# Channel attention and a silu FFN on one core: v's maxima by quarters, halves scaled by two blocks at fixed places, output joins behind subtractions, squares behind copies, the second attention later, decoding held back

## The chip, the cores and the metric

One core of a Trainium2 chip runs one program. The time is device time in microseconds (us) of that core; "before" is the median of 3 runs, and beside it stands one profiled execution, from which all rows below are taken.

## The reference

`q`, `k`, `v` have the shape (2, 6016, 256); `w_in` is 256 x 2048 and `w_out` 2048 x 256.

```python
qn = q / (norm(q, axis=1) + 1e-6);  kn = k / (norm(k, axis=1) + 1e-6)
s  = kn.transpose(0, 2, 1) @ qn / tau          # 256 x 256 for each of two batches
a  = softmax(s, over the last axis)
x  = (v @ a).reshape(12032, 256)
h  = x @ w_in
out = (h / (1 + exp(-h))) @ w_out
```

## The kernel before

The kernel never forms `x`. For each batch it multiplies the softmax `a` into `w_in` ("mixing", `mix`), so that `h` comes from `v` and a mixed 256 x 2048 weight. Both big products use a seven-product scheme on 2 x 2 blocks: sums and differences of the blocks of `v` are called B11, T1, B21, B22, T2, T3, T4, those of the mixed weight A11 to S4. Every factor is split into a high and a low half in f16, so that one product takes three matmuls.

The 12032 tokens are worked in 12 passes `p` of 1024 columns (896 in the last pass of each batch): passes 0 to 5 are batch 0, 6 to 11 batch 1. Passes 0 and 5 are "unpaired" (`emit_pair_group`), and the scheduler orders them. The other ten are "paired": `emit_unit` writes out eight units (u0 to u7 below) of four slots, and there TensorE, VectorE and ScalarE keep the order in which the code is written. A unit goes so:

- slot 0: products into the PSUM banks y (S1 by T1), x (A11 by B11) and z (A12 by B21); ScalarE copies y and x into `c51`; VectorE subtracts z (`g<-c,z`);
- slot 1: y again (S4 by B22), then x again (S2 by T2); ScalarE copies x into `c2` (L797); VectorE subtracts y (`g<-c,y`);
- slot 2: x again (S3 by T3); VectorE subtracts (`g<-x,c`, L767); ScalarE takes the silu of two rows and then of one (L770);
- slot 3: x a fourth time (A22 by T4); ScalarE takes its silu straight from PSUM (`g<-x`), and makes the high half (L777).

There is one bank x, so each product into it waits until ScalarE or VectorE has read the one before. The products of the second layer (L876) are queued in `ready`, and up to `room_left` of them fill each slot. Work that follows a unit is put off by slots with `later` and run by `tail`: the low halves of `hl` (L780), sums for the second layer (L946), and for every fourth unit the output: four copies out of PSUM (`take`, L916), four half-wide joins (`join`, L931), two full-wide joins with their store (`leave`, L935).

After each slot, steps of background work may be written behind it: `scale_v` of the next pass (the maximum of |v|, L148; a power-of-two scale; high halves on ScalarE, L534; low halves on VectorE, L537; subtractions L543 and L559), the matmuls and then the softmax of batch 1's `attention` (the `filler`), the sums of squares of batch 1's q and k (`square_sums`, ScalarE, L266, passes 1 to 3) and the mixing. Which slot takes a step is fixed by small tables in the main loop. In pass 0 the int64 view of the weights is decoded (`decode_wi`, `prepare`: casts on ScalarE, L203, and merges on VectorE, L205) while the first products run.

Of the kernel before, what the change touches and what calls it, by code (L numbers as in the profile page):

```python
# [18 lines left out]
P = 128  # L19
# [11 lines left out]
def channel_attention_then_silu_ffn(ctx, tc, kq, qT, kT, vT, tau, w_in, w_out, outT):  # L31
# [240 lines left out]
    def attention(b):  # L272
# [58 lines left out]
        else:  # L331
# [20 lines left out]
            root = half  # L352
        yield

# [7 lines left out]
        yield  # L362
        rq_ps = small_psum("rq_ps")
        for cb in range(KC):
            diag = sm.tile([P, P], F32, tag="diag", name="diag")
            nc.vector.tensor_scalar(
                out=diag, in0=ident, scalar1=rn[:, cb : cb + 1], scalar2=None, op0=ALU.mult
            )
            nc.tensor.matmul(
                rq_ps[:, cb * P : (cb + 1) * P], ones, diag, start=True, stop=True  # L370
            )
        nc.vector.tensor_scalar(
            out=rn[:, KC:], in0=rn[:, KC:], scalar1=rtau, scalar2=None, op0=ALU.mult
        )
        if b == 0:
# [21 lines left out]
        if b:  # L397
            yield
        yield
# [91 lines left out]
    def scale_v(p):  # L491
# [5 lines left out]
        if p < 2:  # L497
# [34 lines left out]

        def high(o, src):
            nc.scalar.activation(out=m[:, 0, o, :h], in_=src, func=AF.Copy, scale=s)  # L534

        def low(o, src):
            nc.vector.scalar_tensor_tensor(  # L537
                out=m[:, 1, o, :h], in0=src, scalar=s, in1=m[:, 0, o, :h], op0=ALU.mult,
                op1=ALU.subtract,
            )  # L540
# [4 lines left out]
        if p > 1:  # L545
            high(B11, v[0][0])
            sub(t3, v[0][1], v[1][1])
            yield
            low(B11, v[0][0])
            high(B21, v[1][0])  # L550
            yield
            low(B21, v[1][0])
            high(B22, v[1][1])
            yield
            low(B22, v[1][1])
            sub(v[0][1], v[0][0], v[0][1])
            yield
            high(T1, v[0][1])
            nc.vector.tensor_tensor(out=t2, in0=v[1][1], in1=v[0][1], op=ALU.add)  # L559
            yield  # L560
            low(T1, v[0][1])
            high(T3, t3)
            yield
            low(T3, t3)
            sub(t4, t2, v[1][0])
            high(T2, t2)
            yield
            low(T2, t2)
            high(T4, t4)
            yield  # L570
            low(T4, t4)
        if p == 0:
# [110 lines left out]
    def emit_pair_group(p, i):  # L683
# [38 lines left out]
        g11 = minus(c1, z)  # L722
        tail(0)
        yield
        finish(silu(g11, g11, 1, 0))
# [3 lines left out]
        g12 = minus(c2, y)  # L729
        tail(1)  # L730
        yield
        t12 = silu(g12, g12, 1, 1)
        product(x, S3, T3)
        g22 = minus(x, c5)
        finish(t12)
        tail(2)
        yield
        finish(silu(g22, g22, 2, 1))
        product(x, A22, T4)
        finish(silu(x, room("g"), 2, 0))  # L740
        tail(3)
        yield

    def emit_unit(p, u):
# [46 lines left out]
        tail(0)  # L791
        minus(top[:, 0], c51[:, 1], z)
        yield
        product(y, S4, B22)
# [3 lines left out]
        tail(1)  # L798
        minus(top[:, 1], c2, y)
        yield  # L800
        product(x, S3, T3)
        minus(low[:, 1], x, c51[:, 0])
        tail(2)
        silu(top, top)
        silu(low[:, 1], low[:, 1])
        yield
        product(x, A22, T4)
        tail(3)
        silu(x[:, :h], low[:, 0])
        high(tops, top)  # L810
# [9 lines left out]
    def tail(slot):  # L820

        for _, run in sorted(tails.pop(ticks[0], ()), key=lambda x: x[0]):
            run()
        ticks[0] += 1

    def later(slot, *those, order=0):
        tails.setdefault(ticks[0] + slot, []).extend((order, run) for run in those)
# [8 lines left out]
    def out_of_unit(p, u, blocks, rest_top, high_low, rest_low):  # L836
# [281 lines left out]
    with at(0):  # L1118
# [41 lines left out]
        next(sqgen)  # L1160
        filler = attention(1)
    anchor = {}

# [87 lines left out]
    behind(start, anchor, {mybir.EngineType.DVE})  # L1251
    old = None
    fixed = ExitStack()
    for p, (b, n, w) in enumerate(pairs):
# [13 lines left out]
        if n + w == N - pairs[-1][2] and b + 1 < B:  # L1268
            steps(sqgen)
            norms["go"] = True  # L1270
        for i in range(NI):
            if i == (4 if p == 0 else 0) and p + 1 < len(pairs):
                load_v(p + 1)
# [28 lines left out]
            for _ in (emit_unit if p in paired else emit_pair_group)(p, i):  # L1302
                if ahead:
                    behind(start, ahead, {mybir.EngineType.PE})
                    ahead = None
                if p == 0 and i < 2:
                    prepare()
                take = 2 if p == 0 and i > 2 and len(pending) > 4 - slot else 1
                over = p == len(pairs) - 1 and i == NI - 1
                room_left = (8, 12, 16 - 4 * over, 8 - 8 * over)[slot] if p in paired else 12 * take  # L1310
                queue = ready if p in paired else pending
# [7 lines left out]
                if p in paired:  # L1319
                    many = {2: 3, 3: 4, 4: 1, 6: 3, 7: 4}.get(i, 0)  # L1320
                    if slot in ((), (3,), (), (1, 2, 3) if p < 4 else (0, 1, 2), range(4))[many]:
                        vgen = background(vgen)
                elif i >= 1 and vgen is not None and (
                    p == 0 or slot in ((0, 2) if not last else (0, 2, 3) if i > 4 else (2, 3))
                ):
                    vgen = background(vgen, 2 if p == 0 else 1)
# [27 lines left out]
    while tails or ready:  # L1354
        tail(0)
        while ready:
            ready.pop(0)[1]()
# [31 lines left out]
```

## Time and profile before

| what | value |
| --- | --- |
| median of 3 runs | 1034.81 us (1033.71 to 1035.3) |
| profiled execution, its own time | 1034.91 us |
| its span, from the first to the last instruction | 1033.1 us |
| granted TensorE clock, mean | 0.999 |
| TensorE matmul busy | 1006.9 us |
| VectorE busy | 844.1 us |
| ScalarE busy | 799.2 us |
| GpSimd busy | 180.0 us |

Time and span differ by 1.8 us, which lies around the span. Matmuls are pipelined and their ends are modelled, so that the busy share of TensorE is no measure of its useful work; starts are recorded.

### The profile page before, as it was taken

The numbers are of one execution on the slowest core, as the hardware profiler recorded it, in microseconds if no ns is written. First come the engines' busy times: TensorE is split into PE (matmuls) and PEld (weight loads), VectorE is DVE, ScalarE is ACT, GpSimd is POOL, SyncE is SP. The second block draws the span as 40 slices with busy tenths as digits, with TensorE's granted clock in tenths as the row PEclk, the third lists the DMA queues.
The fourth block names the chain that finished last, engine by engine and source line by source line (L and its number), as shares of the span: only waits on it lengthen the run. The fifth ranks groups of instructions, "written<-read, shape, count | busy, mean of one in ns | idle before, by whom it ended". The sixth has DMA issues, their size and how long they took to land.

```text
span 1033.1 us, 20363 instructions
## 1 busy us (share of the span) xinstructions
PE 1006.9 (97%) x8222; PEld 837.5 (81%) x8222; DVE 844.1 (82%) x1359; ACT 799.2 (77%) x1161; POOL 180.0 (17%) x259
## 2 busy tenths in 40 slices
PE   9999999999999999999999999999999999999997
PEld 8876554788888888888655788888888888888997
DVE  6998568689889879879779779878878878879776
ACT  6688687789888888777788678778778778778774
POOL 0011000122212222212000122122112122122231
PEclk9999999999999999999999999999999999999999
DMA  9997010456646646435101235435435435334433
GB/s 368 397 397 243 1 41 1 153 128 178 187 127 186 189 115 166 102 70 150 37 1 43 78 82 125 125 87 128 120 83 131 115 82 145 101 78 123 100 87 74
DMA packets 58064, 132.85 MB, mean 129 GB/s; under 512 B 6258, under 2 KB 18370, under 8 KB 57970
## 3 DMA queue, kind: packets, MB, share of 16 engines
q0 software_dynamic: 27216, 62.08, 25.4%
q1 hardware_dynamic: 30466, 68.95, 19.4%
q8 instruction: 64, 1.05, 0.4%
q10 hardware_dynamic: 288, 0.52, 0.1%
q14 instruction: 30, 0.25, 0.1%
HBM read 57.67 MB, written 12.32 MB: 68 GB/s over the span
## 4 chain that ended last, share of the span: by engine, by line
PE 68%; DVE 13%; ACT 12%; DMA 4%; issue 3%; POOL 0%; DVEq 0%; SPq 0%; ACTq 0%; POOLq 0%
PE o L876 26%; PE x L760 16%; PE y L760 7%; PE o L662 6%; PE sc L301 4%; PE z L760 4%; ACT hl L777 3%; DVE hl L780 2%; DVE g L767 2%; PE x L693 2%; DVE sb L935 1%; PE w L441 1%; DVE av L148 1%; PE y L693 1%; ACT g L770 1%
## 5 line engine op out<-in xcount | busy, mean ns | idle before, releaser
L760 PEld LDWEIGHTS <-wall 128*128 128x128 f16 x3360 | 327.6, 98 | 54.3 <-issue 18.9
L760 PE MATMUL x<-m,wall 128*128 128x256 f16 (+1 forms) x1920 | 259.2, 271 | 13.2 <-DVE g L767 8.0
L780 DVE SCALAR_TENSOR_TENSOR hl<-g,sg,hl 128x1024 f16<-128x1024 f32 (+1 forms) x160 | 203.0, 1269 | 65.8 <-ACT hl L777 63.9
L876 PE MATMUL o<-hl,wo 128*128 128x256 f16 (+1 forms) x1920 | 249.2, 271 | 0.2 <-DVE hl L780 0.2
L876 PEld LDWEIGHTS <-wo 128*128 128x128 f16 x2240 | 218.8, 98 | 24.7 <-issue 1.5
L770 ACT ACTIVATE g<-g,alpha 128x1024 f32<-128x1024 f32 (+3 forms) x160 | 147.5, 927 | 84.9 <-DVE g L767 83.9
L777 ACT ACTIVATE hl<-g,sg 128x1024 f16<-128x1024 f32 (+1 forms) x160 | 181.7, 1136 | 0.0
L953 POOL DMA_DIRECT2D sums<-hl x99 | 85.9, 867 | 291.0 <-DMA sums<-hl 103.9
L760 PE MATMUL y<-m,wall 128*128 128x256 f16 (+1 forms) x960 | 129.7, 271 | 0.1
L662 PE MATMUL o<-hl,wo 128*128 128x512 f16 (+1 forms) x384 | 86.9, 366 | 0.1
L876 PE MATMUL o<-t,ws_lo 128*128 128x256 f16 (+1 forms) x362 | 86.8, 271 | 0.0
L876 PE MATMUL o<-t,ws_hi 128*128 128x256 f16 (+1 forms) x362 | 86.8, 271 | 0.0
L951 POOL DMA_DIRECT2D sums<-hl x40 | 29.4, 735 | 303.0 <-DVE hl L780 123.7
L770 ACT ACTIVATE g<-x,alpha 128x512 f32<-128x512 f32 (+1 forms) x80 | 54.2, 678 | 34.8 <-PE x L760 34.1
L797 ACT COPY c<-x 128x512 f32<-128x512 f32 (+1 forms) x80 | 46.5, 581 | 38.8 <-PE x L760 38.2
L301 PE MATMUL sc<-kq_t 128*128 128x256 f32 x320 | 73.6, 381 | 0.4 <-DMA kq_t<-in_kq 0.4
L767 DVE TENSOR_TENSOR g<-x,c 128x512 f32<-128x512 f32 (+1 forms) x80 | 54.4, 680 | 23.8 <-PE x L760 23.7
L767 DVE TENSOR_TENSOR g<-c,y 128x512 f32<-128x512 f32 (+1 forms) x80 | 54.2, 678 | 23.1 <-ACT c L797 22.8
L946 DVE TENSOR_TENSOR t<-t,hl 128x1024 f16<-128x1024 f16 (+1 forms) x101 | 69.0, 683 | 2.7
L662 PEld LDWEIGHTS <-wo 128*128 128x128 f16 x384 | 37.5, 98 | 39.2 <-issue 0.8
L301 PEld LDWEIGHTS sc<-kq_t 128*128 128x128 f32 x320 | 60.0, 190 | 11.1 <-DMA kq_t<-in_kq 1.9
L876 PEld LDWEIGHTS <-ws_hi 128*128 128x128 f16 x640 | 62.6, 98 | 6.8
(194 smaller groups left out, 1553.8 us busy)
## 6 DMA issues: line engine op xcount, KB each, us to landing
sums<-hl POOLq DMA_DIRECT2D x134, 256.0 KB, 3.3
kq_t<-in_kq SPq DMA_DIRECT2D x39, 512.0 KB, 8.9
sums<-t POOLq DMA_DIRECT2D x54, 256.0 KB, 2.3
v_t<-in_vT SPq DMA_DIRECT2D x10, 1024.0 KB, 6.1
outT<-sb SPq DMA_DIRECT2D x40, 256.0 KB, 3.0
extra<-hl POOLq DMA_DIRECT2D x38, 256.0 KB, 3.5
turned<-in_qT SPq DMA_DIRECT2D x10, 512.0 KB, 4.8
turned<-in_kT SPq DMA_DIRECT2D x10, 512.0 KB, 4.8
```

Source lines behind the costliest of these rows:

```text
L301: nc.tensor.matmul(sc[:, cb, :], t[:, i, 0, cb * P : (cb + 1) * P], t[:, i, 1, :], start=(j + i == 0 and cb == 0), stop=(j + i == J - 1), ...
L662: nc.tensor.matmul(o[:, :h], a[:, f, ee], hl[:, m, :h], start=(c == 1 and i == 0), stop=(c == NF and i == 2),)
L693: nc.tensor.matmul(bank[:, :h], wm[:, u, a - 1], m[:, y, x, :h], start=(first and j == 0), stop=(j == 2), skip_group_check=True,)
L760: nc.tensor.matmul(bank[:, k * wide : (k + 1) * wide], mixed[b, i][:, v, a - 1], m[:, c, x, at : at + wide], start=(first and j + k == 0), ...
L767: nc.vector.tensor_tensor(out=g, in0=a[:, :h], in1=c[:, :h], op=ALU.subtract)
L770: nc.scalar.activation(out=g, in_=src, func=AF.Silu, scale=alpha)
L777: nc.scalar.activation(out=hl[:, :, 0], in_=g, func=AF.Copy, scale=sg)
L780: nc.vector.scalar_tensor_tensor(out=hl[:, :, 1], in0=g, scalar=sg, in1=hl[:, :, 0], op0=ALU.mult, op1=ALU.subtract,)
L797: nc.scalar.copy(c2[:, :h], x[:, :h])
L876: nc.tensor.matmul(o[:, side * wide : (side + 1) * wide], a, x, start=(first and j == 0), stop=(last and j == len(these) - 1), skip_group_ ...
L946: nc.vector.tensor_tensor(out=o, in0=x, in1=y, op=ALU.add)
L953: nc.gpsimd.dma_start(o, y, accum_op=ALU.add)
```

## The change

- `amax_of` of a paired pass's v (p over 1) takes four maxima of 512 columns in place of two of 1024, each at a place of its own, and the differences t3 and T1 are made while the scale is worked out.
- High and low halves are made for two neighbouring blocks at once (`high(B11, first, 2)`), 1024 columns in one instruction, and T4 alone: eight instructions on the two engines take the place of fourteen.
- The slots for these steps come from a table, `V_PLACES`, the same in every paired pass. The next load of `v` is issued from within `scale_v`.
- `leave` runs in the new `tail_end`, behind the unit's subtraction of the slot, and the second `leave` one slot later (10, was 9).
- A square of q or k stands in slot 2 in u0 to u3 and in slot 1 in u4, u6 and u7 (`SQUARES`, passes 1 to 4); before, it stood in slot 0 of every unit of passes 1 to 3.
- The softmax of batch 1 starts in the middle of pass 4 (u4) and not at its start, with some of its steps merged or split otherwise; the last unit of pass 4 has another `room_left`.
- In pass 0, `decode_wi` and `prepare` are held behind the latest instructions of the products on VectorE and ScalarE.

```diff
-            amax = yield from amax_of([t[:, kc, :w] for kc in range(KC)], "av")
-        s, inv = yield from pow2_scale(amax, "v", bufs=2, square=p == 1)
+            quarters = [x for kc in range(KC) for x in v[kc]]
+            maxima = amax_of(quarters, "av")
+            for _ in quarters:
+                next(maxima)
+                yield
...
         if p > 1:
-            high(B11, v[0][0])
             sub(t3, v[0][1], v[1][1])
             yield
...
             sub(v[0][1], v[0][0], v[0][1])
             yield
...
+            next(scale)
+            s, inv = steps(scale)
+            yield
+            first, second = (t[:, kc, :w].rearrange("p (l h) -> p l h", l=2) for kc in range(KC))
+            high(B11, first, 2)
+            yield
+            low(B11, first, 2)
+            yield
             nc.vector.tensor_tensor(out=t2, in0=v[1][1], in1=v[0][1], op=ALU.add)
             yield
+            high(B21, second, 2)
+            yield
+            high(T2, x[:, :2, :h], 2)
+            yield
+            low(B21, second, 2)
+            yield
+            low(T2, x[:, :2, :h], 2)
+            yield
             sub(t4, t2, v[1][0])
+            yield
+            high(T4, x[:, 2:, :h], 1)
+            if p + 1 < len(pairs):
+                load_v(p + 1)
+            yield
+            low(T4, x[:, 2:, :h], 1)
...
     def tail(slot):
-        for _, run in sorted(tails.pop(ticks[0], ()), key=lambda x: x[0]):
-            run()
+        these = sorted(tails.pop(ticks[0], ()), key=lambda x: x[0])
+        after.extend(run for order, run in these if order > 2)
+        for order, run in these:
+            if order < 3:
+                run()
         ticks[0] += 1
+    def tail_end():
+        while after:
+            after.pop(0)()
...
-            later(8, lambda: leave(0), order=2)
-            later(9, lambda: leave(1), order=2)
+            later(8, lambda: leave(0), order=3)
+            later(10, lambda: leave(1), order=3)
...
+    V_PLACES = (
+        (), (0, 2), (3,), (0, 2, 3), (0, 1, 2), (0, 1, 2), (2, 3), (0, 1, 2, 3)
+    )
+    SQUARES = ((2,), (2,), (2,), (2,), (1,), (), (1,), (1,))
...
+                        start = len(traced())
                         steps(decode_wi(j))
+                        behind(start, anchor, {mybir.EngineType.DVE, mybir.EngineType.Activation})
...
-                    many = {2: 3, 3: 4, 4: 1, 6: 3, 7: 4}.get(i, 0)
-                    if slot in ((), (3,), (), (1, 2, 3) if p < 4 else (0, 1, 2), range(4))[many]:
+                    if slot in V_PLACES[i]:
                         vgen = background(vgen)
...
+                if p == closing and (i, slot) == (NI // 2, 1):
+                    steps(sqgen)
+                    norms["go"] = True
                 if filler is not None and b == 0 and (p or i >= 2):
-                    if "go" not in norms or slot < 2:
+                    if "go" not in norms or slot in ((0, 1, 3) if p in paired else (0, 1)):
                         filler = background(filler, 1)
-                if p in (1, 2, 3) and sqgen is not None and slot == 0:
+                if p in paired and b == 0 and "go" not in norms and slot in SQUARES[i]:
                     sqgen = background(sqgen) or iter(())
```

Three places show how instructions move. First VectorE in u2 of a pass of batch 1, from its first `hl` to its last sum, before (`sb<-sb 128x512` is a `leave`, `av<-v_t` a maximum over 1024 columns).

```order
L780 SCALAR_TENSOR_TENSOR hl<-g,sg,hl 128x2x512
L935 TENSOR_TENSOR sb<-sb 128x512
L767 TENSOR_TENSOR g<-c_7360,z 128x512
L148 TENSOR_REDUCE av<-v_t 128x1
L780 SCALAR_TENSOR_TENSOR hl<-g,sg,hl 128x2x512
L935 TENSOR_TENSOR sb<-sb 128x512
L767 TENSOR_TENSOR g<-c_7409,y 128x512
L148 TENSOR_REDUCE av<-v_t 128x1
L767 TENSOR_TENSOR g<-x,c_7360 128x512
L946 TENSOR_TENSOR t_7345<-hl 128x1024
L946 TENSOR_TENSOR t_7345<-t_7345,hl 128x1024
```

The same unit's rows on VectorE in the changed program.

```order
L799 SCALAR_TENSOR_TENSOR hl<-g,sg,hl 128x2x512
L786 TENSOR_TENSOR g<-c_7339,z 128x512
L968 TENSOR_TENSOR sb<-sb 128x512
L799 SCALAR_TENSOR_TENSOR hl<-g,sg,hl 128x2x512
L786 TENSOR_TENSOR g<-c_7386,y 128x512
L786 TENSOR_TENSOR g<-x,c_7339 128x512
L979 TENSOR_TENSOR t_7324<-hl 128x1024
L979 TENSOR_TENSOR t_7324<-t_7324,hl 128x1024
L968 TENSOR_TENSOR sb<-sb 128x512
L148 TENSOR_REDUCE av<-v_t 128x1
```

The second `leave` and the only maximum now stand behind the sums, and nothing of the background is left between the two last subtractions.

Second, ScalarE in u5 of a pass of batch 1, from the copy of x in slot 1 to the high half behind slot 3 (`sb<-o` is a `take`, `g<-x` the silu that frees bank x), before.

```order
L797 COPY c_7760<-x 128x512
L916 ACTIVATE sb<-o,back 128x512
L770 ACTIVATE g<-g,alpha 128x1024
L770 ACTIVATE g<-g,alpha 128x512
L916 ACTIVATE sb<-o,back 128x512
L770 ACTIVATE g<-x,alpha 128x512
L777 ACTIVATE hl<-g,sg 128x2x512
```

And the same stretch in the changed program.

```order
L817 COPY c_7738<-x 128x512
L949 ACTIVATE sb<-o,back 128x512
L789 ACTIVATE g<-g,alpha 128x1024
L789 ACTIVATE g<-g,alpha 128x512
L546 ACTIVATE m<-v_t,sv 128x1024
L949 ACTIVATE sb<-o,back 128x512
L789 ACTIVATE g<-x,alpha 128x512
L796 ACTIVATE hl<-g,sg 128x2x512
```

One 1024-column high half of v (`m<-v_t`) has come in ahead of the third `take` and of the silu of x.

Third, ScalarE in the second unit of pass 0, from the copy of x in slot 0 to the copy of x in slot 1 (`t<-` are casts of the decoding, `x<-w` the mixing), before.

```order
L699 COPY c_688<-x 128x512
L203 CAST t<-raw 128x512
L203 CAST t<-held 128x512
L710 ACTIVATE g<-g,alpha 128x512
L164 ACTIVATE hl<-g,sg 128x512
L203 CAST t<-held 128x512
L451 ACTIVATE x<-w,rows 128x2x128 x2
L164 ACTIVATE wi<-t,swi 128x2x256
L699 COPY c_734<-x 128x512
```

And in the changed program.

```order
L714 COPY c_688<-x 128x512
L203 CAST t<-wall 128x512 x2
L725 ACTIVATE g<-g,alpha 128x512
L164 ACTIVATE hl<-g,sg 128x512
L453 ACTIVATE x<-w,rows 128x2x128 x2
L714 COPY c_734<-x 128x512
```

One cast and one high half of `w_in` no longer stand between the two copies.

## Rows read from the trace of the kernel before

**Rows 1.** The page's first part: busy us, share of the span, instructions.
```profile
PE 1006.9 (97%) x8222; PEld 837.5 (81%) x8222; DVE 844.1 (82%) x1359; ACT 799.2 (77%) x1161; POOL 180.0 (17%) x259
```
**Rows 2.** Whom TensorE waited for: us in total, times, longest us.
```profile
PE x L760 <- DVE g L767: 8.0, 12, 1.2
PE x L760 <- ACT c L797: 4.0, 10, 1.6
PE x L693 <- ACT c L699: 2.3, 2, 2.0
```
**Rows 3.** Timeline: first products of passes 3, 4, 5, 7, u1, u2, pass 8.
```profile
330.03 0.71 PE L760 MATMUL y<-m,wall 128*128 128x256 f16 x5
...
406.11 0.60 PE L760 MATMUL y<-m,wall 128*128 128x256 f16 x4
...
486.51 0.35 PE L693 MATMUL y<-m,wall 128*128 128x448 f16 x1
...
721.87 0.49 PE L760 MATMUL y<-m,wall 128*128 128x256 f16 x3
...
731.26 0.82 PE L760 MATMUL y<-m,wall 128*128 128x256 f16 x6
...
740.65 0.82 PE L760 MATMUL y<-m,wall 128*128 128x256 f16 x6
...
798.72 0.38 PE L760 MATMUL y<-m,wall 128*128 128x256 f16 x2
```
**Rows 4.** Timeline of u1 of pass 7: start us, us, engine, [idle before].
```profile
734.44 1.28 DVE L780 SCALAR_TENSOR_TENSOR hl<-g,sg,hl 128x1024 f16<-128x1024 f32 x1 [0.21 <-ACT hl L777]
...
736.23 0.69 DVE L767 TENSOR_TENSOR g<-c,y 128x512 f32<-128x512 f32 x1 [0.51 <-ACT c L797]
...
737.58 0.69 DVE L767 TENSOR_TENSOR g<-x,c 128x512 f32<-128x512 f32 x1 [0.66 <-PE x L760]
...
738.36 0.72 ACT L770 ACTIVATE g<-g,alpha 128x512 f32<-128x512 f32 x1 [0.27 <-DVE g L767]
...
738.99 0.67 ACT L916 ACTIVATE sb<-o,back 128x512 f32<-128x512 f32 x1
...
739.12 0.82 PE L760 MATMUL x<-m,wall 128*128 128x256 f16 x6
...
739.98 0.69 ACT L770 ACTIVATE g<-x,alpha 128x512 f32<-128x512 f32 x1 [0.32 <-PE x L760]
...
741.30 0.38 PE L760 MATMUL x<-m,wall 128*128 128x256 f16 x2
```
**Rows 5.** Timeline of u2 of pass 7: a maximum, the product behind it.
```profile
747.66 1.21 DVE L148 TENSOR_REDUCE av<-v_t 128x1 f32<-128x1024 f32 x1
...
749.52 0.82 PE L760 MATMUL x<-m,wall 128*128 128x256 f16 x6 [0.85 <-DVE g L767]
```
**Rows 6.** Timeline of u1 of pass 1: a square, the product behind it.
```profile
191.47 1.06 ACT L266 ACTIVATE sq<-turned 128x1024 f32<-128x1024 f32 x1
...
193.15 0.82 PE L760 MATMUL x<-m,wall 128*128 128x256 f16 x6 [1.57 <-ACT c L797]
```
**Rows 7.** Timeline of u4 and u5 of pass 4: softmax on ScalarE, product behind.
```profile
451.21 1.28 ACT L394 ACT_TABLE_LOAD   x1
...
453.61 1.28 ACT L770 ACT_TABLE_LOAD   x1
...
454.91 1.76 ACT L770 ACTIVATE g<-g,alpha 128x1024 f32<-128x1024 f32 x2
...
457.29 0.49 PE L760 MATMUL x<-m,wall 128*128 128x256 f16 x3 [0.83 <-ACT g L770]
```
**Rows 8.** Timeline of pass 0, second unit: copy in slot 1, product behind it.
```profile
85.72 0.58 ACT L699 COPY c<-x 128x512 f32<-128x512 f32 x1
...
86.35 0.81 PE L693 MATMUL x<-m,wall 128*128 128x512 f16 x3 [1.96 <-ACT c L699]
```
**Rows 9.** Groups of VectorE instructions by shape: busy us, mean ns.
```profile
L627 DVE TENSOR_SCALAR back<-back,iwo 128x1 f32<-128x1 f32 x12 | 2.5, 212 | 0.4
```

More of the change, by code (lines that the diff above doesn't have):

```diff
@@ L362, in attention @@
         yield
-        rq_ps = small_psum("rq_ps")
-        for cb in range(KC):
-            diag = sm.tile([P, P], F32, tag="diag", name="diag")
+        diags = [sm.tile([P, P], F32, tag="diag", name="diag") for cb in range(KC)]
+        for cb, diag in enumerate(diags):
             nc.vector.tensor_scalar(
                 out=diag, in0=ident, scalar1=rn[:, cb : cb + 1], scalar2=None, op0=ALU.mult
-            )
-            nc.tensor.matmul(
-                rq_ps[:, cb * P : (cb + 1) * P], ones, diag, start=True, stop=True
             )
@@ L374, in attention @@
         )
+        if b:
+            yield
+        rq_ps = small_psum("rq_ps")
+        for cb, diag in enumerate(diags):
+            nc.tensor.matmul(
+                rq_ps[:, cb * P : (cb + 1) * P], ones, diag, start=True, stop=True
+            )
         if b == 0:
@@ L517, in scale_v @@
             yield
-        else:
-            amax = yield from amax_of([t[:, kc, :w] for kc in range(KC)], "av")
-        s, inv = yield from pow2_scale(amax, "v", bufs=2, square=p == 1)
+        if p < 2:
+            s, inv = yield from pow2_scale(amax, "v", bufs=2, square=p == 1)
+        else:
+            quarters = [x for kc in range(KC) for x in v[kc]]
[3 more added lines that the diff above has]
+                yield
+            next(maxima)
+            amax = steps(maxima)
+            scale = pow2_scale(amax, "v", bufs=2)
+            next(scale)
+            yield
         if m is None:
@@ L531, in scale_v, with high, low @@
         t2, t3, t4 = (x[:, i, :h] for i in range(3))
-        def high(o, src):
-            nc.scalar.activation(out=m[:, 0, o, :h], in_=src, func=AF.Copy, scale=s)
-        def low(o, src):
+        def high(o, src, n):
+            nc.scalar.activation(out=m[:, 0, o : o + n, :h], in_=src, func=AF.Copy, scale=s)
+        def low(o, src, n):
             nc.vector.scalar_tensor_tensor(
-                out=m[:, 1, o, :h], in0=src, scalar=s, in1=m[:, 0, o, :h], op0=ALU.mult,
-                op1=ALU.subtract,
+                out=m[:, 1, o : o + n, :h], in0=src, scalar=s, in1=m[:, 0, o : o + n, :h],
+                op0=ALU.mult, op1=ALU.subtract,
             )
@@ L545, in scale_v @@
         if p > 1:
-            high(B11, v[0][0])
             sub(t3, v[0][1], v[1][1])
             yield
[L549 to L555, printed above, removed]
             sub(v[0][1], v[0][0], v[0][1])
             yield
-            high(T1, v[0][1])
+            next(scale)
+            s, inv = steps(scale)
[5 more added lines that the diff above has]
+            yield
             nc.vector.tensor_tensor(out=t2, in0=v[1][1], in1=v[0][1], op=ALU.add)
             yield
-            low(T1, v[0][1])
-            high(T3, t3)
+            high(B21, second, 2)
             yield
-            low(T3, t3)
+            high(T2, x[:, :2, :h], 2)
[4 more added lines that the diff above has]
+            yield
             sub(t4, t2, v[1][0])
-            high(T2, t2)
             yield
-            low(T2, t2)
-            high(T4, t4)
+            high(T4, x[:, 2:, :h], 1)
+            if p + 1 < len(pairs):
+                load_v(p + 1)
             yield
-            low(T4, t4)
+            low(T4, x[:, 2:, :h], 1)
         if p == 0:
@@ L723, in emit_pair_group @@
         tail(0)
+        tail_end()
         yield
@@ L730, in emit_pair_group @@
         tail(1)
+        tail_end()
         yield
@@ L736, in emit_pair_group @@
         tail(2)
+        tail_end()
         yield
@@ L741, in emit_pair_group @@
         tail(3)
+        tail_end()
         yield
@@ L803, in emit_unit @@
         tail(2)
+        tail_end()
         silu(top, top)
@@ L820, in tail @@
     def tail(slot):
-        for _, run in sorted(tails.pop(ticks[0], ()), key=lambda x: x[0]):
-            run()
+        these = sorted(tails.pop(ticks[0], ()), key=lambda x: x[0])
[3 more added lines that the diff above has]
+                run()
         ticks[0] += 1
+    after = []
+    def tail_end():
+        while after:
+            after.pop(0)()
     def later(slot, *those, order=0):
@@ L1268, in channel_attention_then_silu_ffn @@
         if n + w == N - pairs[-1][2] and b + 1 < B:
-            steps(sqgen)
-            norms["go"] = True
+            closing = p
         for i in range(NI):
             if i == (4 if p == 0 else 0) and p + 1 < len(pairs):
-                load_v(p + 1)
+                if p + 1 not in loaded:
+                    load_v(p + 1)
                 vgen = scale_v(p + 1)
@@ L1306, in channel_attention_then_silu_ffn @@
                 if p == 0 and i < 2:
+                    start = len(traced())
                     prepare()
+                    behind(start, anchor, {mybir.EngineType.DVE, mybir.EngineType.Activation})
                 take = 2 if p == 0 and i > 2 and len(pending) > 4 - slot else 1
                 over = p == len(pairs) - 1 and i == NI - 1
-                room_left = (8, 12, 16 - 4 * over, 8 - 8 * over)[slot] if p in paired else 12 * take
+                held_over = p == closing and i == NI - 1
+                room_left = 12 * take
+                if p in paired:
+                    room_left = (
+                        (8, 12, 12, 0) if over else (8, 8, 12, 16) if held_over else (8, 12, 16, 8)
+                    )[slot]
                 queue = ready if p in paired else pending
@@ L1325, in channel_attention_then_silu_ffn @@
                 ):
-                    vgen = background(vgen, 2 if p == 0 else 1)
+                    vgen = background(vgen, 2 if p == 0 or (i, slot) == (1, 2) else 1)
+                if p == closing and (i, slot) == (NI // 2, 1):
+                    steps(sqgen)
+                    norms["go"] = True
                 if filler is not None and b == 0 and (p or i >= 2):
-                    if "go" not in norms or slot < 2:
+                    if "go" not in norms or slot in ((0, 1, 3) if p in paired else (0, 1)):
                         filler = background(filler, 1)
-                if p in (1, 2, 3) and sqgen is not None and slot == 0:
+                if p in paired and b == 0 and "go" not in norms and slot in SQUARES[i]:
                     sqgen = background(sqgen) or iter(())
```

11 lines of the change are left out of this document (7 added, 4 removed).

## Prediction

> **What bounds the kernel now.** The page's first part shows TensorE busy for 1006.9 us [rows 1], but the ends of matmuls are modelled, so I read starts instead. The list of waits says whom TensorE waits for [rows 2]: VectorE's last subtraction of a unit, 8.0 us in 12 waits; ScalarE's copy of bank x in slot 1, 4.0 us in 10; the same copy in pass 0, 2.3 us in 2. They are short waits spread over the program, so the next view is the timeline, for the rhythm [rows 3]. From u1 to u2 of pass 7 is 740.65 - 731.26 = 9.39 us, and nothing waits there; eight such units would be 75.12 us. Pass 3 takes 406.11 - 330.03 = 76.08 (0.96 over), pass 4 80.40 (5.28 over), pass 7 76.85 (1.73 over). Pass 2 repeats pass 3, and passes 8 and 9 repeat pass 7.
>
> The calm unit shows the slack [rows 4]. VectorE is idle for 0.21, 0.51 and 0.66 us ahead of its last three unit operations. `g<-x,c` ends at 738.27, the product that needs it starts at 739.12: 0.85 us to spare. ScalarE's silu of x ends at 740.67, and the next unit's second product into x starts at 741.30: 0.63 to spare. What is put into a unit beyond these numbers holds TensorE up. In u2 of pass 7 a maximum of 1.21 us stands just ahead of that subtraction, and the product behind starts at 749.52 after 0.85 us idle [rows 5]. In pass 1 a square of 1.06 us stands ahead of the slot-1 copy, and TensorE is idle for 1.57 us [rows 6]. In pass 4 the softmax puts two table loads of 1.28 us into ScalarE's row, and the product behind waits for 0.83 us by the row's idle [rows 7]. In pass 0 casts delay the slot-1 copy, and TensorE is idle for 1.96 us [rows 8].
>
> **The change part by part.** No matmul is added or removed; only the waits can change. The sum is made against the profiled execution's own 1034.91 us, 0.10 above the median.
>
> *Squares.* Moved from slot 0 to slot 1 behind the copy, or to slot 2. In slot 2 a square takes 1.06 us and a little more for reading its sum (0.2, an estimate), against 0.27 and 0.32 of ScalarE's idle and 0.63 to spare [rows 4]: about even, at most 0.1 lost in the one unit that has a `take` too. So the excess of passes 2 and 3 goes (0.96 each), and in pass 1 as much again, and there also the wait at 193.15 less the copy itself (a copy took 0.58 in [rows 8]): 1.57 - 0.58 = 0.99, and some 0.3 in its neighbour, an estimate. 3 x 0.96 + 0.99 + 0.3 = 4.2 us. Bounds: 2 (pass 1 keeps its entry) to 4.2.
>
> *Maxima and joins.* In batch 1 every place at which VectorE was late (u2: two maxima and two `leave`s; u6: a low half and a subtraction behind `g<-c,y`) is emptied by the new table. A quarter maximum is about half of 1.21, 0.65 with a fixed part, and stands behind `g<-c,z`, where 0.21 + 0.51 us are idle [rows 4], or behind the sums, where more is idle. So 1.73 a pass goes in passes 7 to 9; pass 10, whose v is 896 wide, gives 1.73 x 896/1024 = 1.5; pass 6, in which VectorE still finishes mixed weights, 0.3, an estimate. Sum 7.0; bounds 5.5 (half of it stays in the passes beside 7 to 9 and a fifth there) to 7.5.
>
> *A new wait in u5.* This goes against the change. u5 holds three `take`s, and now also a low half of 1024 columns (VectorE, slot 0), the sum t2 (VectorE, slot 1) and a high half of 1024 (ScalarE, slot 2). Rows overlap by about 0.08 (738.36 + 0.72 ends 0.09 after the next start). On VectorE the low half takes 1.28 - 0.08 = 1.20 and the two small `back` operations 2 x 0.21 - 0.05 = 0.37 [rows 9], against 0.21 + 0.51 idle: `g<-c,y` is 0.85 late. t2 takes 0.60 against 0.66 idle: `g<-x,c` is 0.79 late and ends 0.06 before its product, so there nothing is lost. But ScalarE's silu of one row waits for it: 738.36 + 0.79 = 739.15. Then come that silu (0.64), the high half (1.05: two silus of 1024 and 512 take 1.76 together [rows 7], less 0.71), the `take` (0.59) and the silu of x at 741.43, ending at 742.12. The product at 741.30 is late by about 0.8. Nothing else waits longer: the high half queued behind it feeds VectorE, which has its own idle in u6. Seven passes with 1024-wide v (1 to 3, 6 to 9) cost 7 x 0.8 = 5.6, pass 10 some 0.5: 6.1 us. Bounds: 0 (the `take` is ready early and rows overlap more) to 1.46 a pass (the whole 742.12 - 740.67, no slack), 11.7. I take 6.1, since every duration in it is a row's own.
>
> *Attention in pass 4.* The same steps in u4 to u7, in three slots a unit. In u5 two rounds of four small operations (each 4 x 0.21 less overlap, 0.75) come on top of the u5 wait: `g<-x,c` is then some 1.4 beyond its slack and the silu of x 0.5 more, 1.9 in all. u6 0.5, an estimate. The softmax, 454.91 - 451.21 = 3.70 us on ScalarE, lands in u7's slot 1, with T4's high half (0.6) behind it: 0.83 + 0.6 + a 0.3 shortfall of VectorE = 1.7. Sum 4.1 against 5.28: 1.2 us gained. Bounds: 3.3 gained (only softmax costs) to 2 lost.
>
> By the Trainium skill (ScalarE: Activation LUTs, What ACT_TABLE_LOAD costs) a switch costs the 1.283 us load and about 1.38 us of drain, 2.66 together; here the load at 453.61 ends at 454.89 and the silu starts at 454.91 [rows 7], so the row shows no drain. By the page the block would be 2 x 1.38 = 2.76 us longer in u7 and the forecast 1030.0.
>
> *Decoding held back.* A cast (0.65) and a half (0.63, both by the 0.72 row less overlap) leave the stretch ahead of the copy at 85.72 [rows 8]: 1.2 gained, bounds 0 to 1.96. The work comes back in units 3 and 4 of pass 0, hidden under queued second-layer matmuls and attention matmuls; without that cover it would cost two casts and two halves, 2.5 us.
>
> Sum: 4.2 + 7.0 - 6.1 + 1.2 + 1.2 = 7.5, so 1034.9 - 7.5 = 1027.4 us.
>
> **Rivals.** *No wait in u5*: if ScalarE's row has the slack, 6.1 more are gained: 1021.3. For it: u4, u6 and u7 take the same high half without a `take` and should fit. Against: the sum above, from rows.
>
> *Given back by half*: the u5 wait at its upper bound for some passes and pass 4 no better than before: 1031.5. For it: u5 has the fullest rows on both engines, and a late unit starts the next one late.
>
> *Nothing moves*: VectorE and ScalarE do nearly the same work, and each wait reappears at another place: 1034.5. Against: three of the places stand where [rows 4] shows idle time.
>
> *Slower, by one mechanism*: the v halves stand directly ahead of the silu of x in u4, u5, u6 and u7. In u4 and u6 without the third `take` the room is 0.32 + 0.59 + 0.63 = 1.54 against 1.05, a margin of 0.5. If `g<-x,c` is over 0.5 late there too, u4, u5 and u6 each lose 0.8: 9 passes x 3 x 0.8 = 21.6 against 13.6 gained elsewhere, 1043. Against: VectorE has no block of 1.20 in u4.
>
> *The drain of the page above*: 1030.0, hardly likely, as the trace has the load without it.
>
> **How the numbers follow.** A measurement of this kernel can tell about 0.2%, 2.1 us, from no change. Chances: forecast 0.44, no u5 wait 0.20, given back by half 0.20, drain 0.02, nothing moves 0.08, slower 0.06. The time is the forecast's, 1027.4; its own range is 1024.5 to 1030. To leave out no more than 2 in 10, the range goes from 1021 to 1033. Faster than 1032.7: 0.44 + 0.20 + 0.02 and most of the 0.20, 0.85; same 0.08; slower 0.07.
>
> **What would show it.** In the changed profile u2 and u6 of passes 7 to 9 should be 9.39 us, with no wait of TensorE for `g<-x,c` there; u5 should be about 10.2, with a wait of x for the silu of x. Passes 2 and 3 should be near 75.9, pass 4 near 79.2, and the idle at the second unit of pass 0 near 0.7. I am wrong if u5 is 9.39, if pass 4 grows, or if the units with a high half of v all wait for the silu of x.

## Result and the profile after

The changed kernel takes 1026.11 us (median of 4 runs, 1026.03 to 1026.3), the kernel before 1035.05 beside it (4 runs, 1033.71 to 1035.61): a ratio of 0.9916, 95% interval 0.9899 to 0.9933. The forecast was 1027.4. In the later comparisons the kernel before had medians of 1033.9 to 1034.2, so the gain is 8 to 9 us. The profiled execution took 1026.12 us, its span is 1024.4.

The page's first part, to be read against [rows 1]: no engine lost much work; ScalarE has 30 instructions fewer, VectorE 10.

```profile
PE 1004.3 (98%) x8222; PEld 837.6 (82%) x8222; DVE 839.7 (82%) x1349; ACT 792.7 (77%) x1131; POOL 179.4 (18%) x259
```

Whom TensorE waits for after the change (us in total, times, longest):

```profile
PE x L779 <- ACT g L789: 4.7, 9, 0.6
PE x L779 <- ACT c L817: 1.8, 4, 0.7
PE x L708 <- DVE g L719: 1.7, 1, 1.7
PE x L779 <- DVE g L786: 1.5, 2, 0.9
```

Against [rows 2] the waits for VectorE's subtraction fell from 8.0 to 1.5 us and those for the slot-1 copy from 4.0 to 1.8. The first line is nearly new: nine waits for ScalarE's silu of x, where there was one [rows 7]. In pass 0 the wait passed from ScalarE's copy to VectorE's subtraction.

Rows of the changed kernel's timeline, in order of time: pass 0 (85 to 89 us); first products of passes 3 and 4; two late products of pass 4; the table loads at its end; the first product of pass 6; then pass 8 with u2, u3, u5, u6, u7 and the first of pass 9, and between them the end of u5.

```profile
86.57 1.09 DVE L162 TENSOR_TENSOR wall<-x,wall 128x896 f16<-128x896 f32 x1 [0.27 <-ACT wall L161]
...
87.58 0.68 DVE L719 TENSOR_TENSOR g<-x,c 128x512 f32<-128x512 f32 x1
...
88.31 0.81 PE L708 MATMUL x<-m,wall 128*128 128x512 f16 x3 [1.68 <-DVE g L719]
...
328.54 0.49 PE L779 MATMUL y<-m,wall 128*128 128x256 f16 x3
...
404.41 0.49 PE L779 MATMUL y<-m,wall 128*128 128x256 f16 x3
...
460.33 0.82 PE L779 MATMUL x<-m,wall 128*128 128x256 f16 x6 [0.89 <-DVE g L786]
...
463.23 0.81 PE L779 MATMUL x<-m,wall 128*128 128x256 f16 x6 [0.55 <-ACT g L789]
...
479.76 1.28 ACT L789 ACT_TABLE_LOAD   x1
...
481.06 1.76 ACT L789 ACTIVATE g<-g,alpha 128x1024 f32<-128x1024 f32 x2
...
564.70 0.49 PE L779 MATMUL y<-m,wall 128*128 128x256 f16 x3
...
717.10 0.60 PE L779 MATMUL y<-m,wall 128*128 128x256 f16 x4
...
735.88 0.49 PE L779 MATMUL y<-m,wall 128*128 128x256 f16 x3
...
745.27 0.60 PE L779 MATMUL y<-m,wall 128*128 128x256 f16 x4
...
764.10 0.82 PE L779 MATMUL y<-m,wall 128*128 128x256 f16 x6
...
769.90 0.68 DVE L786 TENSOR_TENSOR g<-c,y 128x512 f32<-128x512 f32 x1
...
771.10 0.69 DVE L786 TENSOR_TENSOR g<-x,c 128x512 f32<-128x512 f32 x1
...
772.51 1.13 ACT L546 ACTIVATE m<-v_t,sv 128x1024 f16<-128x1024 f32 x1
...
773.49 0.60 PE L779 MATMUL y<-m,wall 128*128 128x256 f16 x4
...
773.55 0.66 ACT L949 ACTIVATE sb<-o,back 128x512 f32<-128x512 f32 x1
774.12 0.67 ACT L789 ACTIVATE g<-x,alpha 128x512 f32<-128x512 f32 x1
...
774.84 0.81 PE L779 MATMUL x<-m,wall 128*128 128x256 f16 x6 [0.54 <-ACT g L789]
...
783.57 0.49 PE L779 MATMUL y<-m,wall 128*128 128x256 f16 x3
...
792.96 0.60 PE L779 MATMUL y<-m,wall 128*128 128x256 f16 x4
```

Pass 8 takes 792.96 - 717.10 = 75.86 us (76.85 before, [rows 3]). Counted on from pass 6 this is pass 8, and so are the rows that [rows 3] to [rows 5] call pass 7; their "pass 8", at 798.72, is the first product of pass 9. Passes 7 to 9 repeat each other unit by unit in every program here, so no reading hangs on the number. u2 is 745.27 - 735.88 = 9.39: its wait is gone. The new wait stands at 774.84: VectorE's `g<-x,c` starts 771.10 - 764.10 = 7.00 us into u5 (6.32 in the calm unit, [rows 4]), then follow the two silus, the high half of v, the third `take` and the silu of x, which ends at 774.79. The product that waits is the second one of u6, so u5 reads 9.39 by its first products and u6 783.57 - 773.49 = 10.08.

By starts of passes, before minus after:

| stage | gained, us |
| --- | --- |
| pass 0, up to pass 1 | 0.61 |
| pass 1; 2; 3 | 0.68; 0.20; 0.21 |
| passes 4 and 5 | 2.23 |
| pass 6; 7, 8, 9; 10 | -0.15; 0.99 each (2.96); 0.95 |
| pass 11 and the end | 1.0 |

Together 8.7 us, the difference of the spans. The last line was no part of the forecast, and it is chance. This is the row of the kernel before, some 12 us before its end:

```profile
1021.49 0.54 PE L876 MATMUL o<-sums,wo 128*128 128x224 f16 x4 [0.94 <-DMA sums<-hl]
```

TensorE waited there for the last accumulating transfer. The changed kernel has no such wait, but the same wait came back in one of twelve profiled variants (e2, at 1008.66, 1.00 us), whose last pass is the same code; e7 and e10, with the last pass of the kernel before, don't have it. Without this last line the gain is 7.7.

### The profile page after: what moved, and what is told of

Its sections match the earlier page's. It is cut to its first block, busy times and chain, and to the rows that moved or that the text cites. A ratio compares the mean times of both kernels' runs of the same rounds, so it can differ in the third digit from the quotient of the medians.

```text
span 1024.4 us, 20291 instructions
## 1 busy us (share of the span) xinstructions
PE 1004.3 (98%) x8222; PEld 837.6 (82%) x8222; DVE 839.7 (82%) x1349; ACT 792.7 (77%) x1131; POOL 179.4 (18%) x259
## 3 DMA queue, kind: packets, MB, share of 16 engines
q8 instruction: 64, 1.05, 0.4%
## 4 chain that ended last, share of the span: by engine, by line
PE 72%; ACT 11%; DVE 11%; DMA 3%; issue 3%; DVEq 0%; POOL 0%; SPq 0%; ACTq 0%
PE o L909 29%; PE x L779 16%; PE y L779 8%; PE o L677 6%; PE z L779 4%; DMA kq_t<-in_kq 3%; PE sc L301 3%; ACT g L789 3%; DVE hl L799 3%; PE x L708 2%; DVE g L786 2%; PE w L443 1%; ACT hl L796 1%; ACT g L725 1%; PE y L708 1%
## 5 line engine op out<-in xcount | busy, mean ns | idle before, releaser
L986 POOL DMA_DIRECT2D sums<-hl x99 | 86.9, 877 | 324.1 <-DMA sums<-hl 105.6
L984 POOL DMA_DIRECT2D sums<-hl x40 | 25.5, 638 | 285.0 <-DVE hl L799 217.8
L909 PEld LDWEIGHTS <-ws_lo 128*128 128x128 f16 x640 | 62.6, 98 | 6.8
L979 DVE TENSOR_TENSOR t<-hl 128x1024 f16<-128x1024 f16 (+1 forms) x101 | 68.1, 675 | 0.0
```

The source lines that it names most:

```text
L909: nc.tensor.matmul(o[:, side * wide : (side + 1) * wide], a, x, start=(first and j == 0), stop=(last and j == len(these) - 1), skip_group_ ...
L979: nc.vector.tensor_tensor(out=o, in0=x, in1=y, op=ALU.add)
L986: nc.gpsimd.dma_start(o, y, accum_op=ALU.add)
```

## Experiments

**The wait behind u5: two single moves.** One entry of the table moves in each.

```diff
-        (), (0, 2), (3,), (0, 2, 3), (0, 1, 2), (0, 1, 2), (2, 3), (0, 1, 2, 3)
+        (), (0, 2), (3,), (0, 2, 3), (0, 1, 2, 3), (1, 2), (2, 3), (0, 1, 2, 3)   # e1
+        (), (0, 2), (3,), (0, 2, 3), (0, 1, 2), (0, 1), (1, 2, 3), (0, 1, 2, 3)   # e2
```

> The low half of B11 and T1 on VectorE moves from slot 0 of u5 to slot 3 of u4; the high half of 1024 columns stays in slot 2 of u5. Theory: the wait at u6's second product (0.70 us in seven passes, 0.29 in pass 10) needs both, since the subtraction from x in slot 2 of u5 is 0.68 late by the low half (7.00 us behind the unit's start, 6.32 in the calm unit) and the high half of 1.05 then finds no room; without the low half it shrinks to under 0.1. u6 then 9.4 us, the time 1026.1 - 5 = 1021. Rival: ScalarE's high half makes the wait alone; u6 stays at 10.0 to 10.1 and the time at 1026. Second rival: the low half delays VectorE in u5 from its new place as well, and the wait halves: 1023.5.

> The high half of B21 and B22 on ScalarE moves from slot 2 of u5 to slot 1 of u6, behind the copy; the low half stays in slot 0 of u5. Theory (both are needed): the wait behind u5 is gone too, u6 starts on time and passes 7 to 9 take 75.2 us; in passes 1 to 3 a square stands at the same place of u6, and u6 and u7 lose some 0.6 there. About 1022.5. Rival (the high half alone makes the wait): the same for u5. Rival (VectorE's low half alone makes it): 10.08 for u6 stays, time 1026 or more.

e1 took 1020.43 us (ratio to before 0.9869, 0.9853 to 0.9886), e2 1022.11 in one run. The timeline of e1 in u5 of pass 8, its first product and its end:

```profile
760.08 0.82 PE L779 MATMUL y<-m,wall 128*128 128x256 f16 x6
...
766.39 0.69 DVE L786 TENSOR_TENSOR g<-x,c 128x512 f32<-128x512 f32 x1
...
767.81 1.13 ACT L546 ACTIVATE m<-v_t,sv 128x1024 f16<-128x1024 f32 x1
...
769.42 0.67 ACT L789 ACTIVATE g<-x,alpha 128x512 f32<-128x512 f32 x1
769.47 0.82 PE L779 MATMUL y<-m,wall 128*128 128x256 f16 x6
...
770.14 0.81 PE L779 MATMUL x<-m,wall 128*128 128x256 f16 x6
```

u5 starts at 760.08 here, so the subtraction starts at 6.31, the calm unit's offset. The high half and the `take` are where they were, and the silu of x ends at 770.09, 0.05 ahead of its product. u6 is 9.40 and pass 8 75.18. In e2 the high half is gone from u5 and the low half stays: u6 is 9.39, passes 7 to 9 take 75.16, and only passes 1 to 3, where a square shares the place, lose 0.2 to 0.3. So each half alone fits and both together make 0.70. Both rivals that name one engine fell.

**Joins and halves of v, apart.** e4 puts the joins back ahead of the subtractions; its edit stands below. e6 keeps the joins behind and undoes v's steps (maxima of 1024, single halves, places as before); that edit is long and not shown.

```diff
-            later(8, lambda: leave(0), order=3)
-            later(10, lambda: leave(1), order=3)
+            later(8, lambda: leave(0), order=2)
+            later(9, lambda: leave(1), order=2)
```

> The changed kernel with both full-wide joins back ahead of the subtractions of slots 0 and 1. By the idle times of the calm unit (0.21, 0.51, 0.66 on VectorE, then 0.85 to spare) two joins of 0.61 each fit where no maximum stands beside them: u2 stays at 9.39 to 9.5, time 1026 to 1026.5, and what was gained in u2 came from the maxima. Rival: the joins made half of the wait of u2 and u6, and 0.9 us a pass comes back in nine passes: 1034.

> The changed kernel with v's maxima over 1024 columns, single halves and their slots as before. Theory: the wait behind u5 goes (5.2 us back), and two maxima of 1.21 in u2 return, now with the joins behind the subtractions: 1.74 in slot 0 against 0.72 of idle and 1.13 in slot 1 against 0.66, 1.49 late, 0.85 to spare, 0.64 lost; u6 loses some 0.69. Passes 7 to 9 76.4, passes 2 and 3 75.3 to 75.8, time 1026. Rival: with the joins out of the way the maxima fit, passes 7 to 9 75.2 to 75.8 and the time under 1023.

e4 took 1026.33 us, as expected, e6 1022.80. The timeline of e6 in u2 of pass 8, from its first product to that of u3:

```profile
733.12 0.82 PE L766 MATMUL y<-m,wall 128*128 128x256 f16 x6
...
736.00 0.68 DVE L955 TENSOR_TENSOR sb<-sb 128x512 f32<-128x512 f32 x1
736.61 1.21 DVE L148 TENSOR_REDUCE av<-v_t 128x1 f32<-128x1024 f32 x1
...
739.53 1.21 DVE L148 TENSOR_REDUCE av<-v_t 128x1 f32<-128x1024 f32 x1
...
741.38 0.81 PE L766 MATMUL x<-m,wall 128*128 128x256 f16 x6 [0.24 <-DVE g L773]
...
742.91 0.82 PE L766 MATMUL y<-m,wall 128*128 128x256 f16 x6
```

u2 is 9.79 with both wide maxima in it, and u6 is 9.47. In the kernel before u2 was 10.39 (751.04 - 740.65, its own first product and that of u3), with the second join ahead of the subtraction as well, and u6 10.07. Pass 8 in four versions:

| pass 8, us | v as before | v changed |
| --- | --- | --- |
| joins ahead | 76.85 (before) | 75.86 (e4) |
| joins behind | 75.65 (e6) | 75.86 (changed kernel), 75.18 (e1) |

v's steps alone empty u2 and u6, and the joins' move adds nothing to that (e4). The joins' move alone takes 1.20 us of the 1.73 a pass (e6), and v's steps, once the low half is moved too, add 0.47 to that (75.18 in e1). The theory written for e6, 1026 us, fell, and its rival held: with the joins out of the way the wide maxima nearly fit. With the wait behind u5 the new halves are worth less than the old ones: e6, in its one execution, is 3.3 us faster than the changed kernel.

**Squares.** e3 is the changed kernel with squares in slot 0 of every unit of passes 1 to 3, e10 the kernel before with squares moved and nothing else.

```diff
-    SQUARES = ((2,), (2,), (2,), (2,), (1,), (), (1,), (1,))
+    SQUARES = ((0,),) * 8                                             # e3
...
-                if p in paired and b == 0 and "go" not in norms and slot in SQUARES[i]:
+                if p in (1, 2, 3) and slot in SQUARES[i] and sqgen is not None:   # e3
...
-                if p in (1, 2, 3) and sqgen is not None and slot == 0:
+                if p in (1, 2, 3) and sqgen is not None and slot == (2 if i < 4 else 1):   # e10
```

> The changed kernel with the squares back in slot 0 of all units of passes 1 to 3. The prediction's term is 4.2 us: 1030.3. By the traces the move is worth 0.91 in passes 2 and 3 (76.08 against 75.88, with 0.70 of the new wait in the second) and 1.38 in pass 1: 3.2, 1029.3, if the wait of the squares and the wait behind u5 add up; passes 2 and 3 then take 76.8. Rival: the two waits overlap, and passes 2 and 3 go back to 76.1 only: 1027.5.

> The kernel before with nothing but the squares moved behind copies (slot 2 in the first four units, slot 1 in the last four, passes 1 to 3). The prediction's term: passes 2 and 3 lose their 0.96 and fall to 75.1 to 75.2, pass 1 falls by 2.25 to 74.0, time 1034 - 4.2 = 1029.8. Rival: v's low halves and the joins made part of the excess of u5 and u7 (0.35 and 0.57), passes 2 and 3 stay at 75.5 to 76.0 and pass 1 gains its 0.9 at u1 alone: 1032.5.

e3 took 1027.30 us: pass 1 76.23, passes 2 and 3 76.18 each. Its u6 of pass 2 is 10.42: the squares' wait and the wait behind u5 mostly overlap, which was the rival. e10 took 1033.61 in an execution with about 3 us at the lower clock, which cost 1.5 (below); by starts pass 1 fell by 1.45, passes 2 and 3 by 0.18 and 0.28, 1.9 together. Its theory, 1029.8, fell. The rival's times for passes 2 and 3 came (75.90 and 75.79), but not by its mechanism: u5 and u7 lost their excess, and what came back stands in u2 and u3. It is seen in the timeline of u2 of pass 2:

```profile
280.96 0.81 PE L760 MATMUL x<-m,wall 128*128 128x256 f16 x6 [0.32 <-DVE g L767]
281.63 1.04 ACT L266 ACTIVATE sq<-turned 128x1024 f32<-128x1024 f32 x1
```

The wait is now for VectorE's last subtraction in u2, beside the old maxima and joins. In e6, with the joins behind, passes 2 and 3 take 75.29: so squares and joins moved together are worth 0.8 of the 0.96, the squares alone 0.2 to 0.3 (e6 has no square in u5, e10 one). The joins alone, with the squares in slot 0 and v as before, were not tried.

**Attention alone.** e7 is the kernel before with the later start of the second attention and its split steps (`closing`, the filler's slots, `room_left` of the last unit).

> The kernel before with nothing but the second attention's later start and split steps. The prediction's term is 1.2 us in pass 4: passes 4 and 5 together 161.3 and the time 1033.7. In the changed kernel both took 160.29 (162.52 before), with the new wait of u5 in it (1.0 and 0.7); without that wait and with the maxima as before 160 to 161 are expected, time 1032.5 to 1033.7. Rival: the attention steps only paid off by the new places of v's halves, and passes 4 and 5 stay at 162.5.

1031.40 us; passes 4 and 5 take 566.22 - 406.03 = 160.19 by the starts in its timeline, 2.33 less than before. The gain doesn't need v's new places.

**Decoding not held back.** e5 and e9 are the same program.

```diff
-                        start = len(traced())
                         steps(decode_wi(j))
-                        behind(start, anchor, {mybir.EngineType.DVE, mybir.EngineType.Activation})
...
-                    start = len(traced())
                     prepare()
-                    behind(start, anchor, {mybir.EngineType.DVE, mybir.EngineType.Activation})
```

> The changed kernel with the decoding of pass 0 no longer held behind the products. The prediction's term is 1.2 us: 1027.3, and pass 1 would start at 178.3. By the trace the wait only passed from the copy to VectorE's subtraction (1.96 us before, 1.68 after) and 0.5 to 0.6 was gained: pass 1 starts at 177.6 to 177.7, time 1026.7. Rival: pass 0 gained by something else, and nothing changes.

> The changed kernel without the hold on the decoding, once more, as the first execution of it (1028.17 us) had a stretch at the lower clock: behind an idle of 1.97 us TensorE's granted clock was 0.50 from 87.6 to 90.6 us, and matmuls of a pitch of 216 ns took 427. If that is chance, the median is 1026.6 to 1026.9 and the wait at the copy of x alone remains (pass 1 starts at 177.6); if the longer row of casts brings the clock down each time, all executions are near 1028.2 and the hold on the decoding is worth 2 us and not 0.5.

e5 took 1028.17 us; e9's four executions 1027.03, 1026.75, 1028.19 and 1027.12. The windows of e5 in pass 0 (length, then busy us of PE, PEld, DVE, ACT, POOL, granted clock, DMA share, GB/s):

```profile
84.00:87.60 3.60, 1.63 (x8) 1.03 (x7) 3.60 (x11) 3.60 (x8) 0.00 (x0) 0.99 0.58 182
87.60:90.60 3.00, 3.00 (x8) 1.81 (x8) 3.00 (x5) 3.00 (x5) 0.52 (x1) 0.50 0.68 253
```

and the same stretch of the kernel before, with the same idle ahead of it (1.96 us, [rows 8]):

```profile
87.60:90.60 3.00, 2.95 (x14) 2.17 (x14) 3.00 (x6) 3.00 (x5) 0.53 (x1) 1.00 0.98 339
```

In e5 TensorE ran 3 us at 0.50, the 1.2 GHz level, behind an idle of 1.97, and did 8 matmuls in place of 14. So the hold is worth 1027.07 - 1026.11 = 0.96 us by the medians (0.70 by the length of pass 0 in the traces of e9 and of the changed kernel), and in the execution of e5 1.5 more. One of e9's four executions, 1028.19, would fit the lower clock too, but it left no trace.

**The rest of the waits, one after the other.** e8 adds to e1 the move of the first maximum from slot 0 of u1 to slot 2 of u0; e11 adds a mixing step of pass 0 one slot later; e12 adds other attention slots in u4 and u5 of pass 4.

```diff
-        (), (0, 2), (3,), (0, 2, 3), (0, 1, 2, 3), (1, 2), (2, 3), (0, 1, 2, 3)
+        (2,), (2,), (3,), (0, 2, 3), (0, 1, 2, 3), (1, 2), (2, 3), (0, 1, 2, 3)   # e8
-                if p == 0 and i < NI - 1:
+                if p == 0 and i < NI - 1 and (i, slot) != (1, 1):   # e11
-                    if "go" not in norms or slot in ((0, 1, 3) if p in paired else (0, 1)):
+                    if "go" not in norms or slot in ({4: (1, 2, 3), 5: (2, 3)}.get(i, (0, 1, 3)) if p in paired else (0, 1)):   # e12
```

> As the kernel with the low half in u4, and the first maximum of a pass moves from slot 0 of u1 to slot 2 of u0. Theory: in u1 of pass 6 the maximum of 0.68 ahead of the last mixed weights and the low half made the 0.82 us wait of the second layer; without it u1 is 8.6 to 8.9, some 0.8 less, the other passes stay: 1020.2. Rival: u2 of pass 6 then gives it back (before the change u1 was 8.91 and u2 9.37): 1020.8 or more.

> As the kernel with the low half in u4 and the first maximum in u0, and in the second unit of pass 0 one step of the mixing comes a slot later, so that VectorE's subtraction from x stands ahead of the mixed weights (1.09 us, behind a cast of 0.94 on ScalarE). Theory: that step is what TensorE's 1.68 us wait at 88.31 in the changed kernel rests on; the subtraction then starts at 86.3 in place of 87.58 and 1.3 us are gained, 1018.7. Rival: the score matmuls behind it then wait for their data or the next unit for its weights, and the time stays at 1019.9.

> As the kernel with the low half in u4, the first maximum in u0 and the mixing step later, and in pass 4 the attention's two rounds of four small VectorE operations (0.70 us each) leave slots 0 and 1 of u5: the first three small ones go to slot 2 of u4, the first round to slot 3 of u4 and the second to slot 2 of u5, behind the sums. Theory: the rounds are what is left of the waits at u5 (0.58 of excess, the subtraction from x) and behind it (0.72, the silu of x) in pass 4; both shrink to under 0.2, and the time is 1018.6 - 1.1 = 1017.5. Rival: the round at the end of u4 delays the low half at the start of u5 in the same way, and half of it stays: 1018.1.

e8: 1019.98 us. u1 of pass 6 is still 9.50 and its 0.82 us wait for a low half is still there; the 0.4 us come from u2 of pass 1 (9.05, 9.42 in e1). This doesn't clear the maximum. In e8 it only moved up within one unbroken row of VectorE that ends in that low half, so the low half starts 5.45 us into u1 as in the changed kernel. In e6 that row holds no maximum, the low half starts at 4.85, and the wait is 0.23. A maximum and the wait in the changed kernel, then the wait in e6:

```profile
579.12 0.68 DVE L148 TENSOR_REDUCE av<-v_t 128x1 f32<-128x512 f32 x1
...
581.91 0.93 PE L909 MATMUL o<-hl,wo 128*128 128x256 f16 x7 [0.82 <-DVE hl L799]
```

```profile
579.52 0.93 PE L896 MATMUL o<-hl,wo 128*128 128x256 f16 x7 [0.23 <-DVE hl L786]
```

In e6 u1 is 8.91 and u2 9.37, as before the change, so what u1 gains u2 mostly gives back, as the rival said. e11: 1018.60. Its timeline in pass 0:

```profile
85.37 0.68 DVE L719 TENSOR_TENSOR g<-c,y 128x512 f32<-128x512 f32 x1
85.96 0.68 DVE L719 TENSOR_TENSOR g<-x,c 128x512 f32<-128x512 f32 x1
...
86.70 0.81 PE L708 MATMUL x<-m,wall 128*128 128x512 f16 x3 [0.32 <-DVE g L719]
```

Nothing stands between the two subtractions any more and the idle is 0.32 in place of 1.68. e12: 1018.07 (ratio to before 0.9847, 0.9831 to 0.9864), the lowest median of all; its executions overlap with those of e11, and by starts passes 4 and 5 together are 0.71 shorter than there. u5 of pass 4 is 9.39, while the product behind it still waits:

```profile
458.04 0.82 PE L779 MATMUL x<-m,wall 128*128 128x256 f16 x6 [0.41 <-ACT g L789]
```

The round of small steps at the end of u4 delays u5's rows, as the rival said.

## Why the prediction was right, step by step

| term of the sum, us | predicted | measured |
| --- | --- | --- |
| squares | 4.2 | 3.2 here (1.09 net in passes 1 to 3, and 3 x 0.70); alone 1.9 |
| maxima and joins, passes 6 to 10 | 7.0 | 6.8 (e1 against before) |
| wait behind u5 | -6.1 | -5.2 (7 x 0.70 + 0.29) |
| attention, passes 4 and 5 | 1.2 | 2.2 |
| decoding | 1.2 | 0.6 in the trace, 0.96 by medians |
| sum | 7.5 | 7.6 (7.7 by the starts of passes) |

- *The wait behind u5* was right in place, cause and nearly in size. VectorE was forecast 0.85 us late at `g<-c,y` and 0.79 at `g<-x,c`; it was 0.83 and 0.68 late (5.80 and 7.00 us into u5, 4.97 and 6.32 in the calm unit [rows 4]). ScalarE's block of 1.05 then missed its slack by 0.70 where 0.8 was expected. e1 and e2 show that it takes both. The text said that "u5 should be about 10.2" and that 9.39 would prove it wrong; that was a slip of bookkeeping, since its own waiting product is the second one of the next unit, and that unit reads 10.08. The sign "all units with a high half of v wait" did not come: the units behind u4 and u6 read 9.39.
- *Maxima and joins*: 1.73 a pass was forecast and 1.67 came in passes 7 to 9 once the other wait was away (e1), 0.53 in pass 6 (0.3), 1.23 in pass 10 (1.5). Pass 10 had only 76.39 - 75.12 = 1.27 to give, so scaling by the width of v was the wrong source. The sum lumped two edits of which v's alone does it all and the joins' alone 1.20 of 1.73: the four versions of pass 8 show it.
- *Squares* were mis-sized by 1.0, nearly all of it in pass 1. With the 0.70 of the new wait added back, passes 2 and 3 gave 0.9 each of 0.96, but pass 1 gave 1.38 of 2.25. Its u1 gained 0.91 (0.99 was forecast), while "some 0.3 in its neighbour, an estimate" came out as a loss of 0.46: u2 took 9.42 in place of 8.96. The rows of the changed kernel, where u2 starts at 195.55:

```profile
193.18 0.68 DVE L786 TENSOR_TENSOR g<-x,c 128x512 f32<-128x512 f32 x1
...
194.96 1.04 ACT L266 ACTIVATE sq<-turned 128x1024 f32<-128x1024 f32 x1
...
196.00 0.67 ACT L789 ACTIVATE g<-x,alpha 128x512 f32<-128x512 f32 x1
...
196.72 0.81 PE L779 MATMUL x<-m,wall 128*128 128x256 f16 x6 [0.35 <-ACT g L789]
```

It is the mechanism of u5 once more: a quarter maximum makes VectorE's subtraction late, and the square in ScalarE's row then finds no room ahead of the silu of x. Where either of the two is elsewhere the wait is gone and u2 takes 8.91 to 9.09: e8 (maximum moved), e3 (square in slot 0), e6 and e10 (no quarter maximum). That the excess of passes 2 and 3 belonged to the squares alone was wrong too: e10 and e6 show that it goes only when the joins move as well.

- *Attention* was over-priced, so its gain came out too small. By starts of products the lateness in pass 4 is 1.05 and 0.72 us behind u5's rows (1.77 where 1.9 was summed), nothing more in u6 (0.5) and 0.76 in u7 (1.7). In u7 the step that failed is the wait for the silu behind the Exp block (0.83 + 0.6): TensorE waits there for VectorE's subtraction alone. The late silu of x ends at 483.96 and the next product into x, which is one of pass 5, starts at 484.01 without idle, behind other work:

```profile
480.55 0.82 PE L779 MATMUL x<-m,wall 128*128 128x256 f16 x6 [0.60 <-DVE g L786]
...
483.29 0.67 ACT L789 ACTIVATE g<-x,alpha 128x512 f32<-128x512 f32 x1
...
484.01 0.73 PE L708 MATMUL x<-m,wall 128*128 128x448 f16 x3
```

This is read from the trace; no run moved the block alone. For the same reason "pass 4 near 79.2" and "if pass 4 grows" can't be read: products of pass 5 now stand in the last unit of pass 4. By the first of them (479.41) pass 4 takes 75.00 us, by the next product into y (485.73) 81.32. Only the two passes together can be compared, 162.52 before and 160.29 after. Of the drain that the Trainium skill (ScalarE: Activation LUTs, What ACT_TABLE_LOAD costs) adds to a switch, this trace shows nothing: the load at 479.76 lasts 1.28 us and the silu starts at 481.06.

- *Decoding*: of 1.2 us 0.6 came, since the step took "idle near 0.7" for granted without asking what stands next on VectorE. There the mixing step (1.09 us) stood ahead of the subtraction, and the wait moved from 86.35 on ScalarE to 88.31 on VectorE. e11 took it away and gained 1.4.
- The rival "nothing moves" had its truth in pass 6 (-0.15: the new wait ate the gain) and in u1 and u2 there, 8.91 and 9.37 before, 9.50 and 8.91 after: by the rows of e6 above, one quarter maximum moved the lateness from u2 to u1. That is read from two traces; no run took out this maximum by itself.
- Two sums in the prediction are a little off and change nothing: 1027.4 + 2.76 is 1030.2 and not 1030.0, and "only softmax costs" would gain 5.28 - 1.7 = 3.6 and not 3.3.

Forecast and measured time differ by 1.3 us. Of these 1.0 is the chance wait in the profiled execution of before, from which the sum was taken and which the changed kernel didn't have. That the terms add up to within 0.2 us of the 7.7 gained up to pass 11 owes something to errors of both signs: 1.0 too much for squares, 1.0 too little for attention, 0.9 too much for the wait and 0.6 too much for decoding.

## What to carry to other kernels

An in-order unit has a slack on each engine, and two additions that each fit can together hold up the engine that both feed: add up the delay along the row that hands over (VectorE's subtraction to ScalarE's silu to TensorE's bank), not engine by engine. When two edits each remove the same wait, test them apart, since the second may only bring its own cost: here undoing the largest part of the change was 3.3 us faster than keeping it, and keeping it with one step moved by one slot was 5.7 faster. And where a wait is shortened, look in the row of the next engine for what stands ahead of the next hand-over before the gain is written down.

## What was not expected of the hardware

- TensorE's granted clock fell to 0.50 for about 3 us in two of five profiled executions (e5, e10) with an idle of some 2 us at the second unit of pass 0, and stayed at 1.00 in the three others (before, e7, e9) with an idle of the same length. It did so in none of the nine with a shorter or later idle there. The cost is 1.5 us; what decides it stays open.
- The last accumulating transfer of the second layer landed too late by 0.94 and 1.00 us in two of fourteen profiled executions (before, e2), on time in the others.
